# A chunked scan with a split-weight feed-forward: decays of the later units made on TensorE from refilled stacked rows, first outputs of a cell one step later, combination from step 25

## The chip, the cores and the metric

One NeuronCore of a Trainium2 chip runs the whole program. Its engines are named as the profile names them: PE (TensorE matmuls, with PEld for the weight loads), DVE (VectorE), ACT (ScalarE), POOL (GpSimd) and SP (SyncE, which here issues all transfers). The metric is the device time of one execution in microseconds (us). Three runs of the kernel before gave a median of 390.32 us.

## The reference

The inputs are drawn at random: x of shape (4, 8, 768, 32), a decay a between 0.85 and 0.95 for each batch, head and token, B and C with 16 states, and two weight matrices of 256x2048 and 2048x256. The scan works in chunks; between chunks it carries a state. Then every token's 256 values go through two matrix products with a leaky ReLU between them.

```python
log_a = np.log(np.clip(a, 1e-06, 1.0))
for c in range(nc):
    cum = np.cumsum(la, axis=-1)
    L = np.exp(cum[:, :, :, None] - cum[:, :, None, :]) * causal
    M = np.einsum('bhin,bhjn->bhij', Cc, Bc) * L
    y_intra = np.einsum('bhij,bhjd->bhid', M, xc)
    y_inter = np.einsum('bhin,bhnd->bhid', Cc, state) * np.exp(cum)[..., None]
    y[:, :, sl] = y_intra + y_inter
    state = decay_full[:, :, None, None] * state + np.sum(Bx, axis=2)
h = x @ w_in
g = np.maximum(0.01 * h, h)
out = g @ w_out
```

## The kernel before

**Units.** The kernel cuts the sequence into 8 chunks of Q = 96 tokens. One chunk of one batch entry, with its 8 heads, is a unit; there are 32, numbered chunk by chunk. A unit needs its decay tile `lt` (112 x 8 heads x 96: the exponentials of differences of cumulative sums, zero above the diagonal), the score products of B and C (multiplied into `lt` on DVE), the products of `lt` with `xs` that give its output, and, but in the last chunk, the products of `xs` with `bn` that give the next state. ACT copies the state out of PSUM (`stage`), and POOL writes it in four small copies into the rows of the next chunk's `xs`.

**Decays in three ways.** Units 0 to 2 use products of masked logarithms (`decay_direct`). Units 3 to 15 use `decay_pe`: two bf16 matmuls of 384 columns multiply stacked rows `dl` and `dr`. These rows hold a mask and the cumulative sums split in three bf16 parts; the sums come from the DRAM buffer `parts_d` into eight slots (`decay_load`). ACT takes the exponential from PSUM. Units 16 to 31 use another chain: SP broadcasts rows of cumulative sums from the DRAM buffer `crow_d` to all partitions (`decay_rows`), POOL subtracts the column values `ccol` (`decay_sub`, line 270), ACT takes the exponential and POOL zeroes what is above the diagonal (`decay_exp`, lines 278 and 279).

**Three stages.** First come 16 units by themselves. The second stage has 32 steps, which do the feed-forward of the first two of the six tiles of 512 tokens. A step is one block f of 128 hidden columns for one tile: `ffn_in` (line 509) has six matmuls of 512 columns, ACT applies the activation twice (`gh` rounded, `hp` in place), DVE takes the difference (`gl`, line 522), and three steps later `ffn_out` (line 533) accumulates six matmuls in PSUM. The steps form six cells; at a cell's end the sums are added to `ob` on DVE, which frees the two PSUM banks for the next cell's first `ffn_out`. The same steps also decode the weights: `decode` issues two or three DVE passes a step (`PASSES`), five passes and two ACT operations for each of the 16 blocks, and `ffn_in` of a block needs its `wh` and `wl`. At the steps in `PAIR` a `pair_block` does the products of the two earlier units and the scores of two new ones in two PSUM tiles of the pool `ps_c`. The third stage (`two_tiles`, from about 200 us on) does the other four tiles by pairs with a seven-product scheme; `combine` prepares its operands on DVE and POOL.

**Order.** All engines run their instructions in the order in which the program is written. Within a step that order is: rows, subtractions and exponentials of coming units (`early`), `ffn_in`, the second activation, the due decode casts, `gl`, the pair block, the decode passes, the combination, `ffn_out`.

Of the kernel before, what the change touches and what calls it, by code (L numbers as in the profile page):

```python
# [32 lines left out]
WARM = 4  # L33
WARM2 = 4
RAWS = 4
# [23 lines left out]
def scan_ffn(ctx: ExitStack, tc: tile.TileContext, a_l, bc_l, bn_l, x_l, w_l, out_l):  # L59
# [10 lines left out]
    plt = scan.enter_context(tc.tile_pool(name="plt", bufs=6, side="right"))  # L70
# [115 lines left out]
    ccol = const.tile([QE, ncols], F32, name="ccol")  # L186
    erev = const.tile([QE, ncols], F32, name="erev")
    crow = const.tile([128, 2, Q], F32, name="crow")
    parts = const.tile([128, 3, Q], BF16, name="parts")
    crow_d = dram.tile([ncols, Q], F32, name="crow_d")  # L190
    parts_d = dram.tile([128, 3, Q], BF16, name="parts_d")
# [6 lines left out]
    def split_sums(prow):  # L198
        rest = const.tile([128, Q], F32, name="rest")
        nc.tensor.matmul(prow, lhsT=la[:, :128], rhs=upto[:, :Q], start=True, stop=True)  # L200
        nc.vector.tensor_copy(parts[:, 0], prow)
        nc.vector.tensor_tensor(out=rest, in0=prow, in1=parts[:, 0], op=ALU.subtract)
        nc.vector.tensor_copy(parts[:, 1], rest)
        nc.vector.tensor_tensor(out=parts[:, 2], in0=rest, in1=parts[:, 1], op=ALU.subtract)


    def late_sums(one, two):
        for g in range(2):
            nc.tensor.matmul(
                one[:, g * Q:(g + 1) * Q], lhsT=la[:, g * 128:(g + 1) * 128],  # L210
                rhs=upto[:, :Q], start=True, stop=True,
            )
        nc.scalar.copy(crow.rearrange("p g i -> p (g i)"), one[:, :2 * Q])
        nc.sync.dma_start(crow_d.rearrange("(g p) i -> p g i", g=2), crow)
        columns(ccol, upto, AF.Copy, two)
# [31 lines left out]
    def decay_pe(u, space):  # L247
        b = (u - DIRECT) % SLOTS
        for g in range(2):
            nc.tensor.matmul(  # L250
                heads_of(space, g), lhsT=dl[:KD, b], rhs=dr[:KD, b, 4 * g:4 * g + 4],
                start=True, stop=True,
            )
        decay_of(u, space)

    def decay_of(u, space):
# [3 lines left out]
        )  # L260

    def decay_rows(u):
        lt = lts[u] = plt.tile([QE, NH, Q], F32, name="lt")
        rows = crow_d[u * NH:(u + 1) * NH, :].rearrange("r i -> (r i)")
        nc.sync.dma_start(
            lt.rearrange("p h i -> p (h i)"), rows.unsqueeze(0).to_broadcast([QE, NH * Q])
        )

    def decay_sub(u):
        nc.gpsimd.tensor_tensor(  # L270
            out=lts[u], in0=lts[u],
            in1=ccol[:, u * NH:(u + 1) * NH].unsqueeze(2).to_broadcast([QE, NH, Q]),
            op=ALU.subtract,
        )

    def decay_exp(u):
        lt = lts[u]
        nc.scalar.activation(lt, lt, AF.Exp)
        nc.gpsimd.affine_select(  # L279
            out=lt[:Q], in_=lt[:Q], pattern=[[0, NH], [1, Q]], compare_op=ALU.is_ge,  # L280
            fill=0.0, base=0, channel_multiplier=-1,
        )
# [121 lines left out]
    const.tile([128, 336], F32, name="shift0")  # L404
    w_half = [const.tile([128, NF, 2 * DM], F32R, name=n) for n in ("wh", "wl")]
    wh, wl = w_half
    const.tile([128, 416], F32, name="shift")
# [144 lines left out]
    with tc.tile_pool(name="ps_d", bufs=2, space=PSUM, reuse_waits="tile") as ps_d:  # L552
# [15 lines left out]
        split_sums(first[:, 0, :Q])  # L568
        nc.sync.dma_start(parts_d, parts)
# [17 lines left out]
        for u in range(FIRST_UNITS):  # L587
            if u == FIRST_UNITS - 1:
                leads.close()
                pg = ctx.enter_context(tc.tile_pool(name="pg", bufs=LAG + 1))  # L590
# [15 lines left out]
            if v == PE_DECAY - SLOTS - 1:  # L606
                decay_load(DIRECT + SLOTS, PE_DECAY - DIRECT - SLOTS)
            rest()
            c, b = divmod(u, NB)
            if c + 2 <= PE_DECAY // NB:  # L610
# [3 lines left out]
                if b == 2:  # L614
                    fetch_bc(c + 2)
                    fetch_w(c + 1)
                if b == 3:
                    fetch_bn(c + 2)
            if b == 2 and c + 1 < PE_DECAY // NB:
                state_decay(c + 1)  # L620
# [11 lines left out]
    early, late = {}, {}  # L632
# [6 lines left out]
    for u, b in PAIR.items():  # L639
        pair_at[b] = ((u - 2, u - 1) if u > PE_DECAY else (), (u, u + 1))  # L640
# [5 lines left out]
    for c in range(PE_DECAY // NB, NC):  # L646
        b = PAIR[NB * c]
        if NB * c > PE_DECAY:
# [39 lines left out]
    def combine(pair, pools, temps, rhs):  # L688
# [7 lines left out]
        nc.vector.tensor_copy(ab[0][0], a)  # L696
        nc.vector.tensor_tensor(out=t12[:, 0], in0=b[:, 0], in1=a[:, 0], op=ALU.subtract)
        nc.vector.tensor_tensor(out=t34[:, 0], in0=b[:, 1], in1=b[:, 0], op=ALU.subtract)
        nc.gpsimd.tensor_tensor(out=ab[0][1], in0=a, in1=ab[0][0], op=ALU.subtract)
        yield  # L700
        nc.vector.tensor_tensor(out=t12[:, 1], in0=b[:, 1], in1=t12[:, 0], op=ALU.subtract)
        nc.vector.tensor_tensor(out=t34[:, 1], in0=a[:, 1], in1=t12[:, 1], op=ALU.subtract)
        nc.vector.tensor_copy(ab[1][0], b[:, 1])
# [198 lines left out]
```

## Time and profile before

| What | us |
|---|---|
| three runs | 386.65, 390.32, 392.08 |
| the profiled execution, its own time | 390.14 |
| its span, first to last instruction | 388.4 |
| PE busy in the span | 340.4 (88%) |
| DVE busy | 261.3 (67%) |
| ACT busy | 191.0 (49%) |
| POOL busy | 187.4 (48%) |

The page's second part cuts the span in 40 equal slices. Its digits are the busy tenths of each slice, and PEclk is the granted TensorE clock in tenths of full speed. Read the two rows together: where PE shows a 4 or a 5, it waited, and where PEclk falls below 9, it also ran slower.

```profile
PE   7999975998679589579599599999999999999995
PEclk9999995999969879869899899999999999999999
```

The slices from the sixth to the twenty-third are the second stage and the first group of the third.

### The profile page before, as it was taken

Reading aid. Unit: us, or ns where it says so; the run is one execution under the profiler, and the core shown is the slowest. Engines: PE = TensorE matmul, PEld = TensorE weight load, DVE = VectorE, ACT = ScalarE, POOL = GpSimd, SP = SyncE. Lnnn points to the kernel's source line nnn. Section 1 sums busy time; section 2 is a strip of 40 time slices with the busy share of each in tenths; the row PEclk is TensorE's granted clock in tenths of the full one; section 3 lists DMA queues with packets and bytes.
Section 4 is the critical chain, followed back from the end, with each engine's and each line's share of the span. In section 5 each row is a group of like instructions: output and inputs, shape, how many; then the busy total and the mean of one; then the engine's idle time right before and its main releaser. Section 6 shows DMA issues by size and latency. Waiting matters only on the chain.

```text
span 388.4 us, 6367 instructions
## 1 busy us (share of the span) xinstructions
PE 340.4 (88%) x2393; PEld 252.5 (65%) x2393; DVE 261.3 (67%) x379; ACT 191.0 (49%) x365; POOL 187.4 (48%) x268
## 2 busy tenths in 40 slices
PE   7999975998679589579599599999999999999995
PEld 3556543766457468357477477777777787777774
DVE  5349868787877867924866768777666766766552
ACT  3247665355356446423325155554556565566542
POOL 5137875417636728630451638555444555544200
PEclk9999995999969879869899899999999999999999
DMA  5727842392462560000100100000000200000002
GB/s 175 212 86 267 259 146 75 106 296 77 181 194 73 190 183 8 2 0 0 45 11 1 54 2 1 0 2 0 0 2 0 108 3 1 0 3 0 0 2 108
DMA packets 10366, 27.86 MB, mean 72 GB/s; under 512 B 2047, under 2 KB 2271, under 8 KB 10335
## 3 DMA queue, kind: packets, MB, share of 16 engines
q1 hardware_dynamic: 10334, 27.45, 21.6%
q8 instruction: 19, 0.31, 0.3%
q14 instruction: 13, 0.10, 0.1%
HBM read 24.13 MB, written 3.32 MB: 71 GB/s over the span
## 4 chain that ended last, share of the span: by engine, by line
PE 44%; DVE 15%; POOL 4%; issue 3%; ACT 3%; DMA 1%; POOLq 0%; DVEq 0%; ACTq 0%
PE sc L719 15%; PE sc L738 10%; PE op L738 6%; PE hp L719 5%; PE hp L509 4%; PE op L533 3%; DVE u L799 3%; DVE c L800 3%; POOL xs L357 2%; DMA lt<-crow_d 1%; POOL lt L270 1%; DVE wl L450 1%; DVE ob L541 1%; DVE gl L522 1%; POOL lt L279 1%
## 5 line engine op out<-in xcount | busy, mean ns | idle before, releaser
L686 POOL TENSOR_TENSOR sl<-s,sh 128x512 fp32r<-128x512 f32 x16 | 20.9, 1304 | 91.6 <-ACT sh L685 91.6
L751 DVE TENSOR_TENSOR gl<-c,gh 128x512 fp32r<-128x512 f32 x48 | 44.7, 934 | 9.4 <-PE op L738 6.1
L747 ACT ACTIVATE gh<-c 128x512 fp32r<-128x512 f32 x48 | 30.4, 633 | 41.6 <-DVE c L800 18.0
L357 POOL COPY xs<-stage 16x64 f32<-16x64 f32 x112 | 34.8, 311 | 29.7 <-ACT stage L354 22.1
L522 DVE TENSOR_TENSOR gl<-hp,gh 128x512 fp32r<-128x512 f32 x30 | 20.6, 687 | 36.9 <-ACT hp L519 36.7
L533 PE MATMUL op<-gh,wh 128*128 128x512 f32 x64 | 28.4, 443 | 13.6 <-DVE ob L541 12.9
L270 POOL TENSOR_TENSOR lt<-lt,ccol 112x768 f32<-112x768 f32 x16 | 25.1, 1570 | 26.7 <-DMA lt<-crow_d 14.5
L509 PE MATMUL hp<-xh,wh 128*128 128x512 f32 x60 | 26.2, 437 | 9.6 <-ACT wh L443 5.8
L509 PE MATMUL hp<-xh,wl 128*128 128x512 f32 x60 | 26.7, 444 | 9.0 <-DVE wl L450 7.0
L516 ACT ACTIVATE gh<-hp 128x512 fp32r<-128x512 f32 x30 | 17.7, 592 | 31.1 <-PE hp L509 31.1
L748 ACT ACTIVATE c<-c 128x512 f32<-128x512 f32 x48 | 30.4, 633 | 1.5
L719 PE MATMUL sc<-xh,sh 128*128 128x512 f32 x64 | 25.9, 404 | 4.8 <-DVE u L792 4.8
L747 ACT ACTIVATE gh<-hp 128x512 fp32r<-128x512 f32 x16 | 9.6, 598 | 40.9 <-PE hp L719 40.9
L799 DVE TENSOR_TENSOR u<-sc,kept 128x512 f32<-128x512 f32 x16 | 11.1, 692 | 27.6 <-PE sc L719 27.6
L533 PE MATMUL op<-gh,wl 128*128 128x512 f32 x64 | 26.9, 421 | 0.0
L533 PE MATMUL op<-gl,wh 128*128 128x512 f32 x64 | 26.8, 419 | 0.0
L671 POOL TENSOR_TENSOR w<-wh,wl 128x512 f32<-128x512 f32 x16 | 26.5, 1656 | 0.0
L309 DVE TENSOR_TENSOR lt<-sc,lt 112x384 f32<-112x384 f32 x32 | 16.3, 550 | 14.6 <-PE sc L304 11.2
L533 PEld LDWEIGHTS op<-gh,wh 128*128 128x128 f32 x64 | 13.1, 204 | 19.9 <-issue 6.4
L719 PE MATMUL sc<-xl,sh 128*128 128x512 f32 x64 | 25.3, 396 | 0.6 <-DVE xl L709 0.6
L738 PE MATMUL sc<-gh,wh 128*128 128x512 f32 x64 | 25.2, 393 | 0.5 <-DVE ob L732 0.5
L738 PE MATMUL op<-gh,wh 128*128 128x512 f32 x64 | 25.4, 397 | 0.0
(160 smaller groups left out, 921.4 us busy)
## 6 DMA issues: line engine op xcount, KB each, us to landing
raw<-w_l SPq DMA_DIRECT2D x16, 512.0 KB, 3.7
lt<-crow_d SPq DMA_DIRECT2D x16, 336.0 KB, 5.2
bc<-bc_l SPq DMA_DIRECT2D x8, 608.0 KB, 5.0
xs<-x_l SPq DMA_DIRECT2D x8, 384.0 KB, 5.2
out_l<-ob SPq DMA_DIRECT2D x12, 256.0 KB, 2.0
bn<-bn_l SPq DMA_DIRECT2D x8, 231.0 KB, 5.1
la<-a_l SPq DMA_DIRECT2D x1, 96.0 KB, 1.9
crow_d<-crow SPq DMA_DIRECT2D x1, 96.0 KB, 1.9
```

The source lines that it names most:

```text
L270: nc.gpsimd.tensor_tensor(out=lts[u], in0=lts[u], in1=ccol[:, u * NH:(u + 1) * NH].unsqueeze(2).to_broadcast([QE, NH, Q]), op=ALU.subtract,)
L357: nc.gpsimd.tensor_copy(to[:, :, hh], stage[hh * D:hh * D + N])
L509: nc.tensor.matmul(hp, lhsT=w_half[half][:, f, k * 128:(k + 1) * 128], rhs=x[t][:, k, :], start=(n == 0), stop=(n == 5),)
L522: nc.vector.tensor_tensor(out=gls[s], in0=hps.pop(s), in1=ghs[s], op=ALU.subtract)
L533: nc.tensor.matmul(op, lhsT=w_half[half][:, f, DM + m * 128:DM + (m + 1) * 128], rhs=x, start=(first and i == 0), stop=(last and i == 2),)
L671: nc.gpsimd.tensor_tensor(out=w32, in0=wh[:, 2 * p:2 * p + 2, :DM], in1=wl[:, 2 * p:2 * p + 2, :DM], op=ALU.add,)
L719: nc.tensor.matmul(bank, lhsT=w[h], rhs=x[g], start=start and i == 0, stop=i == 2, skip_group_check=True,)
L738: nc.tensor.matmul(outs[t][m], lhsT=w_half[half][:, f, DM + m * 128:DM + (m + 1) * 128], rhs=x, start=first and i == 0, stop=last and i == 2,)
L747: nc.scalar.activation(gh, h, AF.Prelu, alpha=0.01)
L748: nc.scalar.activation(in_place, h, AF.Prelu, alpha=0.01)
L751: nc.vector.tensor_tensor(out=gl, in0=g, in1=gh, op=ALU.subtract)
L799: nc.vector.tensor_tensor(out=u3, in0=B, in1=kept, op=ALU.add)
```

## The change

The second chain of decays goes away. `crow_d`, `crow`, `ccol`, `late_sums`, `decay_rows`, `decay_sub` and `decay_exp` are removed. The cumulative sums of all 32 units are split in bf16 parts at the start, in operations twice as wide, and go to a `parts_d` of twice the size. All units from 3 on use `decay_pe`; after each fourth unit, `decay_load` refills its four slots of `dl` and `dr` from DRAM. For units 16 to 31 `pair_decays` issues the four matmuls and two exponentials one step before the pair block, in the two tiles of `ps_c`.

All pair blocks come two steps earlier, the last one and the combination three steps earlier. In a step the decode passes now stand before the pair block. The first `ffn_out` of a cell (but the first cell) is held for one step and issued with the next one. `combine` no longer uses POOL: DVE does the subtractions, ACT the rounding copies. The pools change: `plt` from 6 to 4 buffers, raw weights from 4 to 3, `pg` from 4 to 5; the two spacer tiles become one of 448 columns. Two more dummy matmuls stand at the start and four more before the first `decay_direct`.

```diff
-WARM = 4
+WARM = 6
-RAWS = 4
+RAWS = 3
+SHIFT = 448
+LOAD = 4
-PE_DECAY = 16
-PAIR = {16: 4, 18: 7, 20: 10, 22: 13, 24: 16, 26: 19, 28: 22, 30: 25}
-LAST_OUT = 28
-COMBINE = 28
+PAIR = {16: 2, 18: 5, 20: 8, 22: 11, 24: 14, 26: 17, 28: 20, 30: 23}
+LAST_OUT = 25
+COMBINE = 25
...
-    plt = scan.enter_context(tc.tile_pool(name="plt", bufs=6, side="right"))
+    plt = scan.enter_context(tc.tile_pool(name="plt", bufs=4, side="right"))
...
     def split_sums(prow):
...
+                prow[:, g], lhsT=la[:, g * 128:(g + 1) * 128], rhs=upto[:, :Q],
+                start=True, stop=True,
...
         decay_of(u, space)
+        after_u = u + SLOTS - LOAD + 1
+        if (u - DIRECT + 1) % LOAD == 0 and after_u < NU:
+            decay_load(after_u, min(LOAD, NU - after_u))
...
-        nc.sync.dma_start(parts_d, parts)
+        nc.sync.dma_start(parts_d.rearrange("(g r) t i -> r g t i", g=2), parts)
...
+        keep_warm(second[:, 1], WARM2)
         decay_direct(0, pds[0])
         decay_of(0, pds[0])
         columns(erev, after, AF.Exp, second[:, 0])
-        late_sums(second[:, 1], first[:, 1])
...
-                pg = ctx.enter_context(tc.tile_pool(name="pg", bufs=LAG + 1))
+                pg = ctx.enter_context(tc.tile_pool(name="pg", bufs=LAG + 2))
...
+    def pair_decays(u):
+        spaces = [score_tile(), score_tile()]
+        for e in range(2):
+            decay_pe(u + e, spaces[e])
...
-        for e in range(2):
-            at(early, b - 4 + e, decay_rows, u + e)
-            at(early, b - 3 + e, decay_sub, u + e)
-            at(early, b - 2 + e, decay_exp, u + e)
+        at(decays, b - 1, pair_decays, u)
...
-        nc.vector.tensor_copy(ab[0][0], a)
+        nc.scalar.copy(ab[0][0], a)
...
-        nc.gpsimd.tensor_tensor(out=ab[0][1], in0=a, in1=ab[0][0], op=ALU.subtract)
...
+        nc.vector.tensor_tensor(out=ab[0][1], in0=a, in1=ab[0][0], op=ALU.subtract)
...
         ffn_low(s)
+        decode(n)
         if s in pair_at:
             pair_block(*pair_at[s])
-        decode(n)
+        for f, args in decays.get(s, ()):
+            f(*args)
...
         if s >= LAG:
-            ffn_out(s - LAG)
+            outs_due.append(s - LAG)
+        if rested or not outs_due or steps[outs_due[0]] not in firsts or outs_due[0] == 0:
+            while outs_due:
+                ffn_out(outs_due.popleft())
+            rested = False
+        else:
+            rested = True
```

Three places show how the order moves. In the rows, the names stand for tiles, with a number for each buffer; the line is that of the helper which issues the row.

ACT, between two pair blocks of the second stage, before: a row with `lt` as output and input is the exponential of one unit, whose input POOL has just subtracted.

```order
L359 COPY x32_1143<-sc_1098 128x2x96
L545 COPY ob0_1163<-op_972 128x512
L278 ACTIVATE lt_1054<-lt_1054 112x768
L516 ACTIVATE gh_1180<-hp_1173 128x512
L519 ACTIVATE hp_1173<-hp_1173 128x512
L412 ACTIVATE w32_1189<-raw_947 128x512
L278 ACTIVATE lt_1082<-lt_1082 112x768
L516 ACTIVATE gh_1212<-hp_1205 128x512
```

The same stretch of ACT now, from the end of one pair block to the step before the next.

```order
L333 COPY x32_1095<-sc_1198 128x2x96
L489 ACTIVATE gh_1269<-hp_1262 128x512
L492 ACTIVATE hp_1262<-hp_1262 128x512
L416 CAST wh_142<-w32_1132 128x512
L489 ACTIVATE gh_1298<-hp_1291 128x512
L492 ACTIVATE hp_1291<-hp_1291 128x512
L385 ACTIVATE w32_1307<-raw_1130 128x512
L254 ACTIVATE lt_1314<-sc_1310 112x768
L254 ACTIVATE lt_1320<-sc_1311 112x768
L489 ACTIVATE gh_1335<-hp_1328 128x512
```

The two exponentials no longer stand ahead of the activations of two steps, waiting for POOL; they stand together, behind a step's activations, and read PSUM tiles that PE fills.

DVE around the pair block, before: `gl` of the step, four multiplications of scores into `lt`, then two decode passes.

```order
L522 TENSOR_TENSOR gl_1092<-hp_1084,gh_1091 128x512
L394 TENSOR_TENSOR lt_951<-sc_1097,lt_951 112x384
L394 TENSOR_TENSOR lt_981<-sc_1097,lt_981 112x384
L394 TENSOR_TENSOR lt_951<-sc_1098,lt_951 112x384
L394 TENSOR_TENSOR lt_981<-sc_1098,lt_981 112x384
L423 TENSOR_SCALAR w32_1072<-w32_1072 128x512
L450 TENSOR_TENSOR wl_143<-w32_1014,wh_142 128x512
```

DVE around a pair block now, with a step of three decode passes.

```order
L495 TENSOR_TENSOR gl_1186<-hp_1178,gh_1185 128x512
L403 SCALAR_TENSOR_TENSOR w32_1132<-raw_950,w32_1132 128x512
L410 SCALAR_TENSOR_TENSOR w32_1132<-raw_950,w32_1132 128x512
L390 TENSOR_SCALAR w32_1194<-w32_1194 128x512
L368 TENSOR_TENSOR lt_1161<-sc_1197,lt_1161 112x384
L368 TENSOR_TENSOR lt_1165<-sc_1197,lt_1165 112x384
L368 TENSOR_TENSOR lt_1161<-sc_1198,lt_1161 112x384
L368 TENSOR_TENSOR lt_1165<-sc_1198,lt_1165 112x384
```

The decode passes moved ahead of the four multiplications, for which ACT's copies of `stage` and `x32` wait.

PE at the first output of the second cell, before: the last `ffn_in` row of a step and the cell's first `ffn_out` rows, into the banks `op_1192` and `op_1193`, which the cell before must have left.

```order
L509 MATMUL hp_1173<-xl_445,wh_142 128x512
L533 MATMUL op_1192<-gh_1038,wh_142 128x512
L533 MATMUL op_1192<-gh_1038,wl_143 128x512
L533 MATMUL op_1192<-gl_1039,wh_142 128x512
L533 MATMUL op_1193<-gh_1038,wh_142 128x512
```

PE at the same output now: the scores of the pair block, then the next step's `ffn_in`, then the cell's first output.

```order
L359 MATMUL sc_1198<-bc_966 112x192 x4
L482 MATMUL hp_1262<-xh_443,wh_142 128x512
L482 MATMUL hp_1262<-xh_443,wl_143 128x512
L482 MATMUL hp_1262<-xl_444,wh_142 128x512
L482 MATMUL hp_1262<-xh_443,wh_142 128x512
L482 MATMUL hp_1262<-xh_443,wl_143 128x512
L482 MATMUL hp_1262<-xl_444,wh_142 128x512
L506 MATMUL op_1277<-gh_1041,wh_142 128x512
```

Six matmuls and the pair block moved between the end of the old cell and the first output of the new one.

More of the change, by code (lines that the diff above doesn't have):

```diff
@@ L184, in scan_ffn @@
     nc.vector.tensor_copy(upto_b, upto)
-    ccol = const.tile([QE, ncols], F32, name="ccol")
     erev = const.tile([QE, ncols], F32, name="erev")
[L188 to L191, printed above, removed]
+    parts = const.tile([128, 2, 3, Q], BF16, name="parts")
+    rest = const.tile([128, 2, Q], F32, name="rest")
+    parts_d = dram.tile([ncols, 3, Q], BF16, name="parts_d")
     def columns(to, mask, func, space):
@@ L198, in split_sums @@
     def split_sums(prow):
[L199 to L207, printed above, removed]
         for g in range(2):
             nc.tensor.matmul(
-                one[:, g * Q:(g + 1) * Q], lhsT=la[:, g * 128:(g + 1) * 128],
-                rhs=upto[:, :Q], start=True, stop=True,
-            )
-        nc.scalar.copy(crow.rearrange("p g i -> p (g i)"), one[:, :2 * Q])
-        nc.sync.dma_start(crow_d.rearrange("(g p) i -> p g i", g=2), crow)
-        columns(ccol, upto, AF.Copy, two)
+                prow[:, g], lhsT=la[:, g * 128:(g + 1) * 128], rhs=upto[:, :Q],
+                start=True, stop=True,
+            )
+        nc.vector.tensor_copy(parts[:, :, 0], prow)
+        nc.vector.tensor_tensor(out=rest, in0=prow, in1=parts[:, :, 0], op=ALU.subtract)
+        nc.vector.tensor_copy(parts[:, :, 1], rest)
+        nc.vector.tensor_tensor(
+            out=parts[:, :, 2], in0=rest, in1=parts[:, :, 1], op=ALU.subtract
+        )
     lts = {}
```

64 lines of the change are left out of this document (22 added, 42 removed).

## The prediction

> **What bounds it.** I read the windows by stage first. Their columns are the stretch, its length, and the busy time of PE, PEld, DVE, ACT and POOL (with instruction counts), then the granted clock.
>
> ```profile
> core 0: us, PE busy (x) PEld busy (x) DVE busy (x) ACT busy (x) POOL busy (x), PEclk, DMA share, GB/s
> 69.00:200.70 131.70, 106.29 (x911) 80.48 (x912) 93.31 (x129) 60.17 (x124) 66.55 (x91) 0.90 0.30 98
> 50.00:69.00 19.00, 11.93 (x63) 7.74 (x63) 13.92 (x20) 10.26 (x20) 11.85 (x20) 0.73 0.39 123
> 200.70:388.40 187.70, 175.61 (x739) 137.76 (x737) 122.81 (x163) 95.97 (x164) 82.23 (x87) 0.99 0.04 15
> ```
>
> The third stage is nearly all PE (175.6 of 187.7 us, clock 0.99). The second stage from its fifth step on (69 to 200.7) is not: PE stands still for 131.7 - 106.3 = 25.4 us, and the clock is 0.90. So the stage is bound by what PE waits for. The waits name it, for PE and then for ACT between 50 and 205 us (total, times, longest):
>
> ```profile
> PE op L533 <- DVE ob L541: 12.9, 3, 5.6
> PE hp L509 <- DVE wl L450: 7.0, 6, 2.5
> ```
>
> ```profile
> ACT lt L278 <- POOL lt L270: 22.1, 12, 3.0
> ACT stage L354 <- DVE lt L394: 16.7, 11, 3.3
> ```
>
> PE waits for DVE (weights, and `ob` that frees the banks), but DVE isn't full, and ACT waits 22.1 us for POOL's subtractions. The groups by line in that stretch show POOL's share and a stretched DVE pass:
>
> ```profile
> L270 POOL TENSOR_TENSOR lt<-lt,ccol 112x768 f32<-112x768 f32 x14 | 22.1, 1576 | 25.5 <-DMA lt<-crow_d 13.4 <-PE sc L385 5.9 <-PE op L533 4.1
> L357 POOL COPY xs<-stage 16x64 f32<-16x64 f32 x48 | 16.2, 337 | 11.2 <-ACT stage L354 6.3 <-issue 2.8
> L279 POOL TENSOR_SCALAR_AFFINE_SELECT lt<-lt 96x768 f32<-96x768 f32 x14 | 14.1, 1010 | 9.1 <-ACT lt L278 7.7 <-DVE w L417 1.0
> ```
>
> ```profile
> L437 DVE SCALAR_TENSOR_TENSOR w<-raw,w 128x512 uint32<-128x512 uint32 x11 | 13.9, 1265 | 0.4
> ```
>
> One case from the timeline, start and duration first: POOL waits 6.66 us for the rows from DRAM, ACT's exponential waits for POOL, the step's activation stands behind it, and `gl` comes 3.87 us late.
>
> ```profile
> 86.81 1.47 POOL L270 TENSOR_TENSOR lt<-lt,ccol 112x768 f32<-112x768 f32 x1 [6.66 <-DMA lt<-crow_d]
> ```
>
> ```profile
> 88.31 0.85 ACT L278 ACTIVATE lt<-lt 112x768 f32<-112x768 f32 x1 [2.54 <-POOL lt L270]
> 89.06 0.58 ACT L516 ACTIVATE gh<-hp 128x512 fp32r<-128x512 f32 x1
> ```
>
> ```profile
> 90.16 0.69 DVE L522 TENSOR_TENSOR gl<-hp,gh 128x512 fp32r<-128x512 f32 x1 [3.87 <-ACT hp L519]
> ```
>
> The second cost of POOL is on DVE. A pass beside POOL's subtraction takes 2.69 us; passes beside POOL's small copies take 0.42 and 0.68.
>
> ```profile
> 74.85 2.69 DVE L437 SCALAR_TENSOR_TENSOR w<-raw,w 128x512 uint32<-128x512 uint32 x1
> ```
>
> ```profile
> 75.53 1.47 POOL L270 TENSOR_TENSOR lt<-lt,ccol 112x768 f32<-112x768 f32 x1
> ```
>
> ```profile
> 114.19 1.95 DVE L394 TENSOR_TENSOR lt<-sc,lt 112x384 f32<-112x384 f32 x4 [1.50 <-issue]
> 116.05 0.42 DVE L423 TENSOR_SCALAR w<-w 128x512 uint32<-128x512 uint32 x1
> 116.39 0.68 DVE L450 TENSOR_TENSOR wl<-w,wh 128x512 fp32r<-128x512 f32 x1
> ```
>
> ```profile
> 115.63 3.48 POOL L357 COPY xs<-stage 16x64 f32<-16x64 f32 x8 [2.80 <-issue]
> ```
>
> Last the clock. After a wait of 2.01 us, matmuls start 0.24 us apart; after one of 3.74 us they start 0.43 apart.
>
> ```profile
> 56.39 0.50 PE L509 MATMUL hp<-xh,wl 128*128 128x512 f32 x1 [2.01 <-POOL wl L472]
> 56.72 0.40 PE L509 MATMUL hp<-xl,wh 128*128 128x512 f32 x1
> 56.96 0.39 PE L509 MATMUL hp<-xh,wh 128*128 128x512 f32 x1
> ...
> 61.56 0.80 PE L509 MATMUL hp<-xh,wh 128*128 128x512 f32 x1 [3.74 <-ACT wh L443]
> ...
> 63.84 0.63 PE L509 MATMUL hp<-xl,wh 128*128 128x512 f32 x1
> 64.27 0.63 PE L509 MATMUL hp<-xh,wh 128*128 128x512 f32 x1
> ```
>
> **The change, part by part.** The sum is made against the profiled execution: span 388.4, its time 390.14, so 1.74 lie around the span. It stands 0.2 under the median of 390.32.
>
> *Second stage, from 69 us.* At the slow clock I count some 44 feed-forward matmuls, between these two, each 0.20 us late:
>
> ```profile
> 107.87 0.79 PE L509 MATMUL hp<-xh,wl 128*128 128x512 f32 x1 [2.54 <-DVE wl L450]
> ```
>
> ```profile
> 195.07 0.56 PE L509 MATMUL hp<-xh,wh 128*128 128x512 f32 x1
> ```
>
> That is 8.8 us, and one pair block, which takes 1.9 at full speed (from its first products to the next output) and 3.3 here, adds 1.4:
>
> ```profile
> 80.12 0.54 PE L321 MATMUL sc<-lt,xs 112*32 112x96 f32 x16
> ...
> 82.04 0.50 PE L533 MATMUL op<-gh,wh 128*128 128x512 f32 x1
> ```
>
> Together 10.2; 0.10 x 131.7 = 13.2 bounds it from above. PE's work at full speed is so 106.3 - 10.2 = 96.1. The 14 units 18 to 31 now add two decay matmuls each:
>
> ```profile
> L250 PE MATMUL pd<-dr,dl 123*112 123x384 bf16 x26 | 7.3, 363 | 0.0
> ```
>
> Two in a row can't cost more than 2 x 0.36 us a unit (10.2 in all), nor less than 384/512 of a spacing of 0.23 (4.8). They follow each other without a wait, so I take the lower end with a little for switching: 5.5. SP loses its broadcasts from 52 us on and gets six refills, three of them here; a refill is issued once PE has used the four slots, and is needed six steps later, at least 6 x 12 x 0.23 = 16 us. That hides it; without this cover it would be a landing of some 4 us. ACT's exponentials stay as many and as long; they lose the wait for POOL. POOL loses L270 and L279 (36.2 of its 66.6 us in the stretch), and with them goes the stretching of DVE: L437 alone lost 11 x (1.27 - 0.69) = 6.4.
>
> What is late next? (a) A weight block that is decoded in the step before its use. For block 9, `ffn_in` of step 13 ends, two activations take 1.2, `gl` 0.69, two passes 0.42 and 0.68: 3.0 us, and DVE comes up to 0.7 later from the steps before. PE has meanwhile only the decays (0.8), since the cell's first output is held: the hold, which is meant against the 12.9 us, costs a wait of up to 2.8 here. Block 14 the same way: 0.7. Block 15 needs two passes, ACT's cast (0.6) and one more pass behind four multiplications: 2.7. (b) The new order on DVE: decode passes ahead of the multiplications delay ACT's `stage` copies, and behind these stands the next step's activation. From one pair block to the next, three steps on, ACT's path is 1.2 + 0.69 + 1.5 (passes) + 1.95 (multiplications) + 0.5 (copies), then 2 x 1.2 for two steps, 1.3 for decode operations and 2 x 0.85 for exponentials: some 11.2 us, an estimate. PE needs 36 x 0.23 + 1.9 + 0.8 + 0.4 = 11.4. That is a tie; I take 2 us in all. (c) Slow clock after such waits: 1. Together 9; bounds are 3 (PE always fed) and 20. The hold's own gain, the 12.9, is part of the 25.4. Result: 96.1 + 5.5 + 9 = 110.6 for 131.7, a gain of 21.1.
>
> A rule beside (c): the Trainium skill (TensorE: Matmul & The Clock Gate, Part 1) has the array's clock halve after about 3.4 us of idleness. The rows with 2.01 and 3.74 agree. By that rule my waits, none over 2.8, would cost no slow clock, and the sum would be 1 us less.
>
> *50 to 69 us.* PE waits here for the first weights. The decays of unit 17 need the PSUM tile in which step 1's activations lie, so step 2 starts some 2 us later; the decode chain loses POOL's stretching and sets the end. I take 0, between -4 (PE waits 7.1 in the 19) and +3.
>
> *Start.* PE loses the sums that only the old chain needed:
>
> ```profile
> 9.56 1.17 PE L209 MATMUL sc<-upto,la 96*128 96x96 f32 x4 [0.47 <-ACT erev L196]
> ...
> 10.52 1.09 PE L195 MATMUL sc<-la,upto 96*112 96x256 f32 x2
> ```
>
> They hold it from 9.56 to about 11.5. Four dummies before `decay_direct` give 0.9 to 1.7 back (0.23 or 0.43 each), the second matmul of the split a little more. The doubled DVE splits and the larger store end long before the first stacked decays at unit 3. I take -0.5, between -2 and +1.
>
> *Third stage.* At its second group, DVE adds two `ob`, copies, subtracts, and is caught by POOL's subtraction:
>
> ```profile
> 213.58 1.28 DVE L541 TENSOR_TENSOR ob<-op,ob 128x512 f32<-128x512 f32 x2
> ...
> 215.98 2.83 DVE L698 TENSOR_TENSOR x<-x 128x512 f32<-128x512 f32 x1
> ```
>
> ```profile
> 215.54 2.72 POOL L699 TENSOR_TENSOR xl<-x,xh 128x1024 fp32r<-128x1024 f32 x1 [4.28 <-DVE xh L696]
> ```
>
> ```profile
> 219.46 0.80 PE L719 MATMUL sc<-xh,sh 128*128 128x512 f32 x1 [4.31 <-DVE u L792]
> ```
>
> Before `u` DVE now has two `ob` and two subtractions of 0.69, 2.7 us where it had 1.28 + 2 x 0.68 + 2.83 = 5.5. So the wait of 4.31 falls to 1.5, and eight matmuls at the slow clock (1.6) go too: -4.4. The five later groups exchange POOL's subtractions for DVE's of 1 to 1.4 us, and ACT gets a copy of about 1.2 ahead of `kept` (an estimate, twice 0.6 for twice the columns); PE has other products in between. I take -4.5 in all, between -6 and +3.
>
> Sum: 388.4 - 21.1 + 0 - 0.5 - 4.5 = 362.3; with 1.74 the time is 364.0.
>
> **Rivals.** *ACT and DVE take over.* The tie of (b) breaks: each of some seven three-step periods takes 1 to 2.5 us more than PE needs. For it speak ACT's 16.7 us behind the multiplications, against it that two `hp` buffers let PE run a step ahead. It gives 364 + 7 to 17 = 371 to 381.
>
> *The change doesn't free DVE.* POOL keeps 66.6 - 40 = 26 us of work in the stretch, with the copies (16.2). If all of it held DVE alike, 26/66 of the 25.4 + 10.2 us would stay: 14, so 378; with all the waits for weights kept as well, 386. The rows at 115.63 and 116.39 speak against it. The Trainium skill (GPSIMD Engine Reference, Key points) speaks for it: GpSimd shares its SBUF interfaces with VectorE and contends with its two-input instructions, whatever GpSimd runs. Here the pass of two inputs at 116.39 took 0.68 beside copies, so the trace bears the rule out for subtractions only.
>
> *Slower: SP's queue.* A refill that waits for PE holds the raw weights behind it.
>
> ```profile
> raw<-w_l SPq DMA_DIRECT2D x16, 512.0 KB, 3.7
> ```
>
> With landings of 3.7 us and 16 us of lead it is hidden. To lose the whole gain of 26 us, each of the three would have to cost PE 9 us, by a landing of over 25. From there on the time is over 390, and 400 at 12 us each.
>
> **How the numbers follow.** Forecast 0.66, with 352 to 371 as its own range. A second stage in which PE is always fed, six of the nine us of waits less and the third stage at its lower bound, gives 364 - 6 - 1.5 = 356 and less: 0.06. ACT and DVE 0.13; DVE not freed 0.12; SP 0.03. The predicted time is the forecast's, 364.0. The range 352 to 378 leaves out some 0.2: most of the third case, the end of the second, the last, and a little below. About 2% is what a measurement of this kernel can tell from no change, so the bounds are 382.5 and 398: faster 0.66 + 0.06 + 0.11 + 0.05 = 0.88, same 0.09, slower 0.03.
>
> **What would show it.** Right: from 69 us to the third stage about 111 us with a clock over 0.95; no wait of PE for `ob` over 1 us; L437's successor at 0.69; a wait near 2.8 us before step 14 and one before step 25; in the third stage no wait over 2 us. Wrong: ACT waiting for multiplications over 20 us (first rival), passes over 1 us beside copies (second), PE waiting for `dl` or `dr` (third).

## The result, and the profile after

The changed kernel takes 352.80 us (median of 352.28 to 353.37), the kernel before 389.31 in the same runs; the ratio is 0.906, with an interval of 0.899 to 0.913. So it is faster by 9.4%, where 6.7% was forecast: the time lies at the lower end of the range of 352 to 378. Runs of one kernel differ by up to 11 us (the kernel before took 381.04 to 392.28 in one set of runs), in part by whether the first 25 us go at full or at half speed, so the ratios given for the later runs compare the quicker runs of both kernels. The changed kernel's median comes from the first set alone, so where a few us matter I compare stage lengths from the profiles. They vary less, but they vary: the third stage, the same program in both, took 183.35 us in the run `pair_first` and 186.11 in `pool_sel`.

The profiled execution of the changed kernel has a span of 351.2 us. The page's row of PE shows where it still waits, in the slices with a 5 or a 7 (the last is the end of the program):

```profile
PE   8999957999979998799979999999999999999995
PEclk9999988899999999899998999999999999999999
```

The windows by stage, of the kernel before and then of the changed one. The stages end where the first `ffn_in` starts, where step 4 starts, where the third stage's first product starts, and at the end of the span.

```profile
0.00:50.15 50.15, 46.62 (x681) 26.49 (x682) 31.43 (x70) 24.64 (x57) 26.90 (x72) 1.00 0.63 198
50.15:68.11 17.96, 11.22 (x63) 7.54 (x63) 12.88 (x18) 10.26 (x20) 11.74 (x19) 0.74 0.36 112
68.11:200.70 132.59, 106.99 (x913) 80.67 (x913) 94.20 (x130) 60.17 (x124) 66.55 (x91) 0.89 0.30 99
200.70:388.40 187.70, 175.61 (x739) 137.76 (x737) 122.81 (x163) 95.97 (x164) 82.23 (x87) 0.99 0.04 15
```

```profile
0.00:42.04 42.04, 39.36 (x683) 23.38 (x683) 31.14 (x70) 24.47 (x55) 27.19 (x73) 1.00 0.72 224
42.04:58.76 16.72, 11.74 (x82) 7.93 (x82) 11.54 (x21) 10.20 (x20) 6.67 (x14) 0.90 0.25 88
58.76:167.21 108.45, 101.60 (x925) 79.64 (x925) 72.87 (x127) 62.91 (x128) 21.38 (x61) 0.97 0.24 81
167.21:351.20 183.99, 175.11 (x739) 137.84 (x737) 124.57 (x160) 98.69 (x168) 81.14 (x85) 0.99 0.04 15
```

| Part | before, us | after, us | measured | predicted |
|---|---|---|---|---|
| start and first units | 50.15 | 42.04 | -8.1 | -0.5 |
| steps 0 to 3 | 17.96 | 16.72 | -1.2 | 0 |
| steps 4 to 31 | 132.59 | 108.45 | -24.1 | -21.1 |
| third stage | 187.70 | 183.99 | -3.7 | -4.5 |
| span | 388.40 | 351.20 | -37.2 | -26.1 |

In steps 4 to 31 PE stands still for 108.45 - 101.60 = 6.9 us where it was 25.6. The waits of PE there (total, times, longest) no longer name `ob` or `gl`; what is left are weights, at four places. The first is the border of step 4, with 0.88 us just ahead of the stretch and 1.00 in it. The timeline shows the other three, the steps 14, 24 and 25 (start and duration first, the wait in brackets).

```profile
PE hp L482 <- ACT wh L416: 3.9, 3, 1.8
PE hp L482 <- DVE wl L423: 3.8, 4, 1.3
```

```profile
98.08 0.49 PE L482 MATMUL hp<-xh,wh 128*128 128x512 f32 x1 [1.22 <-ACT wh L416]
99.90 0.50 PE L482 MATMUL hp<-xh,wl 128*128 128x512 f32 x1 [1.32 <-DVE wl L423]
...
139.03 0.50 PE L482 MATMUL hp<-xh,wl 128*128 128x512 f32 x1 [1.23 <-DVE wl L423]
...
144.99 0.50 PE L482 MATMUL hp<-xh,wh 128*128 128x512 f32 x1 [1.81 <-ACT wh L416]
145.71 0.50 PE L482 MATMUL hp<-xh,wl 128*128 128x512 f32 x1 [0.22 <-DVE wl L423]
```

DVE's groups in the same stretch, after: the pass whose mean was 1265 ns at L437 takes 692 at L410, and `wl`, 1033 ns before, takes 684.

```profile
L403 DVE SCALAR_TENSOR_TENSOR w<-raw,w 128x512 uint32<-128x512 uint32 x11 | 8.5, 774 | 0.0
L423 DVE TENSOR_TENSOR wl<-w,wh 128x512 fp32r<-128x512 f32 x12 | 8.2, 684 | 0.7 <-ACT wh L416 0.7
L410 DVE SCALAR_TENSOR_TENSOR w<-raw,w 128x512 uint32<-128x512 uint32 x11 | 7.6, 692 | 0.4
```

The largest surprise is the start. Here are PE's rows there, first of the kernel before, then of the changed one:

```profile
5.46 2.77 PE L231 MATMUL pd<-lt,after 96*112 96x384 f32 x4
...
18.87 2.77 PE L231 MATMUL pd<-lt,after 96*112 96x384 f32 x4
...
23.93 0.89 PE L250 MATMUL pd<-dr,dl 123*112 123x384 bf16 x2
24.61 0.45 PE L111 MATMUL sc<-idle 128*128 128x512 bf16 x1
25.00 0.59 PE L304 MATMUL sc<-bc 32*112 32x192 f32 x8
```

```profile
5.88 1.28 PE L112 MATMUL sc<-idle 128*128 128x512 bf16 x4
7.00 1.46 PE L224 MATMUL pd<-lt,after 96*112 96x384 f32 x4
...
16.03 0.53 PE L243 MATMUL pd<-dr,dl 123*112 123x384 bf16 x2
```

The same four matmuls of 384 columns take 2.77 us in one kernel and 1.46 in the other. Before, PE ran at half speed until 24.6 us; now until about 6.5, inside the four new dummies (four take 1.28 us here, 1.89 at the start of the kernel before, and 1.03 in the run `best_a`, where they begin at full speed). The granted clock doesn't say so: it reads 1.00 in both first windows above. Here only the duration of one shape, compared between two places, gives the speed away.

### The profile page after: what moved, and what is told of

It reads as the page before. It is cut to its first block, busy times and chain, and to the rows that moved or that the text cites. A ratio compares the mean times of both kernels' runs of the same rounds, so it can differ in the third digit from the quotient of the medians.

```text
span 351.2 us, 6281 instructions
## 1 busy us (share of the span) xinstructions
PE 327.8 (93%) x2427; PEld 248.8 (71%) x2427; DVE 240.1 (68%) x375; ACT 196.3 (56%) x371; POOL 136.4 (39%) x232
## 4 chain that ended last, share of the span: by engine, by line
PE 76%; DVE 15%; ACT 4%; POOL 2%; issue 2%; ACTq 0%; POOLq 0%; DVEq 0%
PE sc L694 17%; PE sc L713 12%; PE hp L482 10%; PE op L506 10%; PE op L713 7%; PE hp L694 6%; DVE u L774 3%; DVE c L775 3%; PE sc L278 2%; PE sc L112 2%; DVE lt L368 2%; PE sc L295 2%; PE pd L295 1%; DVE gl L495 1%; PE sc L243 1%
## 5 line engine op out<-in xcount | busy, mean ns | idle before, releaser
L331 POOL COPY xs<-stage 16x64 f32<-16x64 f32 x112 | 29.7, 266 | 79.3 <-ACT stage L328 52.5
L726 DVE TENSOR_TENSOR gl<-c,gh 128x512 fp32r<-128x512 f32 x48 | 50.3, 1070 | 1.9 <-ACT c L723 1.3
L654 POOL TENSOR_TENSOR s<-w 128x128 f32<-128x128 f32 x32 | 23.5, 736 | 17.5 <-PE sc L295 16.3
L482 PE MATMUL hp<-xh,wh 128*128 128x512 f32 x60 | 24.7, 411 | 4.1 <-ACT wh L416 3.9
L482 PE MATMUL hp<-xh,wl 128*128 128x512 f32 x60 | 24.6, 411 | 4.1 <-DVE wl L423 4.1
L694 PE MATMUL sc<-xh,sh 128*128 128x512 f32 x64 | 25.4, 397 | 2.2 <-DVE u L767 2.2
L506 PE MATMUL op<-gh,wh 128*128 128x512 f32 x64 | 27.1, 424 | 0.0
L713 PE MATMUL op<-gh,wh 128*128 128x512 f32 x64 | 25.4, 397 | 0.0
L713 PE MATMUL op<-gh,wl 128*128 128x512 f32 x64 | 25.4, 397 | 0.0
L713 PE MATMUL op<-gl,wh 128*128 128x512 f32 x64 | 25.4, 396 | 0.0
L506 PE MATMUL op<-gh,wl 128*128 128x512 f32 x64 | 25.3, 395 | 0.0
L506 PE MATMUL op<-gl,wh 128*128 128x512 f32 x64 | 25.1, 392 | 0.0
```

The costliest lines, as they stand in the source:

```text
L331: nc.gpsimd.tensor_copy(to[:, :, hh], stage[hh * D:hh * D + N])
L482: nc.tensor.matmul(hp, lhsT=w_half[half][:, f, k * 128:(k + 1) * 128], rhs=x[t][:, k, :], start=(n == 0), stop=(n == 5),)
L506: nc.tensor.matmul(op, lhsT=w_half[half][:, f, DM + m * 128:DM + (m + 1) * 128], rhs=x, start=(first and i == 0), stop=(last and i == 2),)
L654: nc.gpsimd.tensor_tensor(out=s32[:, i], in0=x, in1=y, op=op)
L694: nc.tensor.matmul(bank, lhsT=w[h], rhs=x[g], start=start and i == 0, stop=i == 2, skip_group_check=True,)
L713: nc.tensor.matmul(outs[t][m], lhsT=w_half[half][:, f, DM + m * 128:DM + (m + 1) * 128], rhs=x, start=first and i == 0, stop=last and i == 2,)
```

## The experiments

**The start.** Three runs ask whether the dummies made the 8 us, or the removal of the sums that PE needed there. First the changed kernel with the dummies of before:

```diff
-WARM = 6
+WARM = 4
-WARM2 = 4
+WARM2 = 0
```

> The changed kernel with its dummies as before (four at the start, none ahead of the first decay_direct). Theory (the dummies bring PE to full speed at 7 us where it came at 24): the products of the first units take twice as long again (the four at decay_direct 2.8 us, not 1.46), the first ffn_in comes near 50 us and not at 42, and the time is 359.5 to 361. Rival (the sums that PE no longer makes at the start, and what waited for them, gave the 8 us): 352 to 354, with decay_direct at 1.46.

Measured: 355.60 us median, but of runs from 352.27 to 360.51. The profiled run is the one of 360.51, and it has the slow start:

```profile
4.29 1.17 PE L199 MATMUL sc<-upto,la 96*128 96x96 f32 x4 [0.49 <-ACT la L533]
...
16.77 2.77 PE L224 MATMUL pd<-lt,after 96*112 96x384 f32 x4
...
48.89 0.50 PE L482 MATMUL sc<-xh,wh 128*128 128x512 f32 x1 [0.16 <-DVE lt L283]
```

So the theory's case came in this run. The other three have no trace, but 352.27 can hardly hold a start that costs 7 us, so it did not come in all. Neither range that I had written is right. By these times the start without the dummies is sometimes slow and sometimes not. Then with the two at the start only:

```diff
-WARM2 = 4
+WARM2 = 0
```

> The changed kernel with six dummies at the start but none ahead of the first decay_direct. If the speed needs work without a gap from 1.3 us on, the two at the start suffice, since they fill the wait of 0.5 us ahead of the sums: 351.5 to 353.5. If it needs the stretch from 5.9 to 7 us filled, the start is slow as before: 358 to 361.

Measured: 350.70 us median (349.67 to 357.39). The profiled run is at full speed some 1.3 us sooner than the changed kernel, and its first `ffn_in` comes at 41.44 and not 42.04. What the four dummies cost where they aren't needed doesn't follow from that, since runs that have them reach the first `ffn_in` between 41.06 (`pool_sub`) and 42.59 (`pair_first`):

```profile
5.18 0.49 PE L217 MATMUL pd<-later,upto_b 96*112 96x384 bf16 x2
5.51 1.45 PE L224 MATMUL pd<-lt,after 96*112 96x384 f32 x4
```

But one run of the four, which has no trace, took 7.7 us more than the quickest. Last the dummies alone in the kernel before:

```diff
-WARM = 4
+WARM = 6
...
+        keep_warm(second[:, 1], 4)
         decay_direct(0, pds[0])
```

> The kernel before with the new dummies alone (six at the start, four ahead of the first decay_direct). Theory (dummies): the first ffn_in comes near 42 to 44 us and the time falls by 6 to 8 to 381 to 384. Rival (late_sums held PE and set the slow start): 389 to 391, or 390 plus the dummies' own 1 us.

Measured: 384.87 us (383.48 to 390.09) against 392.62 for the kernel before, measured beside it, a ratio of 0.980 (0.974 to 0.985). In the profiled run the first `ffn_in` comes at 43.60, and the sums at L209, still there, take 0.69 us after a wait of 0.74. So the dummies bring 7.8 us in the median without any other part of the change, and the sums, which are still there, aren't the cause. With six and four dummies all four runs of the changed kernel lie within 1.1 us; here one of the four took 390.09 us all the same, and has no trace. The profiles of all these experiments say it more plainly: in each of the eleven kernels with six dummies at the start PE reaches full speed between 4.4 and 7.4 us, in the three with four dummies (the kernel before, `start_none`, `hold_before`) between 21.9 and 24.6.

**The hold.** The changed kernel without it:

```diff
-        if rested or not outs_due or steps[outs_due[0]] not in firsts or outs_due[0] == 0:
+        if True:
```

> The changed kernel without the hold: a cell's first output is issued in its own step. Theory (the hold covers the additions of ob): PE waits again for ob at the four later borders of cells, some 2 us each since DVE is freer than before (there 3.3 to 5.6), and gets back the 2.5 us at step 14, where it has outputs to do: 355 to 360. Rival (freeing DVE alone brought the additions in time): 350 to 353, no wait for ob over 1 us.

Measured: 353.02 us (349.67 to 353.44), and 124.99 us from the first `ffn_in` to the third stage where the changed kernel has 125.17. The rival held, nearly: three waits for `ob`, the longest 1.1 us, and in their stead less waiting at step 14 (0.3 us), but 3.2 at step 25 where 1.8 stood. In this kernel the hold brings nothing that these runs show.

```profile
PE hp L482 <- ACT wh L416: 4.9, 3, 3.2
...
PE op L506 <- DVE ob L514: 1.5, 2, 1.1
...
PE op L506 <- DVE ob L520: 0.8, 1, 0.8
```

So I gave the hold to the kernel before, alone (its diff is that of the change, with `pg` at `LAG + 2`):

> The kernel before with the hold alone (and one pg buffer more, which it needs). In the kernel before the stretch from the first ffn_in to the third stage took 150.6 us, with waits for ob of 12.9. If the hold is a cure for late additions of ob, whatever makes them late, those waits go and the stretch falls by 8 to 14 us, weights taking 2 to 4 of it back: 137 to 143 us, time 377 to 384 by the start. If the additions are late because DVE is stretched and the same lateness then shows in the weights, as the run without the hold suggests, the waits move to wh and wl and the stretch stays within 4 us: 147 to 151 us.

Measured: the stretch from the first `ffn_in` to the third stage fell from 150.55 to 190.03 - 49.22 = 140.81 us, by 9.7, as the first theory said. From step 4 on all waits for `ob` went (12.9 before), and waits for weights rose, `wh` from 2.0 to 4.9 and `wl` from 6.1 to 9.0, more than the 2 to 4 us that this theory named:

```profile
PE hp L509 <- DVE wl L450: 9.0, 6, 2.6
PE hp L509 <- DVE gl L522: 5.0, 4, 2.3
PE hp L509 <- ACT wh L443: 4.9, 3, 4.4
```

The medians are 383.61 and 391.37, but the ratio is only 0.990 (0.982 to 0.998). The third stage of the profiled run took 3.4 us more than before (191.07 for 187.70), with a new wait of 2.82 for `xl`. The hold and the rest of the change cure the same lateness, so what each is worth depends on the other: 9.7 us of the stage in the kernel before, nothing in the changed one. That the new decays are what makes the difference is likely by the next runs, but no run adds them alone.

**POOL's work beside DVE.** These two runs put back half of the old decays each, without their waits: POOL works on a tile of its own (it takes the spacer's place), two operations for each pair block, and nobody waits for it.

```diff
-    const.tile([128, SHIFT], F32, name="shift")
...
+    def pool_work():
+        nc.gpsimd.tensor_tensor(
+            out=spare, in0=spare, in1=take.unsqueeze(2).to_broadcast([QE, NH, Q]), op=ALU.subtract,
+        )
...
+        for e in range(2):
+            at(early, b - 1 + e, pool_work)
```

> The changed kernel with sixteen subtractions added on POOL, of the size that the kernel before had there (112 x 768 f32, two inputs), on a tile that nothing else reads or writes. They leave the output as it is, and nothing waits for them. Theory (what the old decays cost was above all DVE's passes stretched beside POOL's subtractions): DVE's decode passes rise from 0.69 towards 1.3 us where they meet, weights and ob come late, and the second stage grows by 5 to 15 us: 358 to 368. Rival (it was the wait of ACT and DVE for POOL's results): the passes may stretch, but the time stays at 352 to 354.

Measured: 365.27 us (364.61 to 365.73), 12.5 more, and 136.75 us from the first `ffn_in` to the third stage, 11.6 more. DVE's groups from step 4 on:

```profile
L402 DVE SCALAR_TENSOR_TENSOR w<-raw,w 128x512 uint32<-128x512 uint32 x11 | 10.9, 987 | 0.0
L422 DVE TENSOR_TENSOR wl<-w,wh 128x512 fp32r<-128x512 f32 x12 | 10.7, 896 | 0.7 <-ACT wh L415 0.7
...
L395 DVE TENSOR_SCALAR w<-w 128x512 uint32<-128x512 uint32 x11 | 7.9, 721 | 0.0
L389 DVE TENSOR_SCALAR w<-w 128x512 f32<-128x512 f32 x11 | 7.1, 649 | 0.0
```

The passes rose from 774 to 987, 684 to 896, 490 to 721 and 420 to 649 ns, and PE waits 9.0 us for `wl` where 4.1 stood. Passes that met no large operation of POOL kept their 0.68 and 0.42 us, so the missing spacer tile isn't the cause, and PE waits for nothing of POOL's. So work on POOL that nobody waits for costs 11.6 us here, nearly half as much as the 25.4 us that this stretch gained: 6.8 of PE standing still (136.75 - 118.17 us, against 125.17 - 113.34), the rest in matmuls that take longer, at a clock of 0.93 for 0.96. Then the selection, with `affine_select` on 96 x 768 in place of the subtraction:

> The same with POOL's other operation of the old decays, the selection of 96 x 768 f32 with one input, on a tile of its own. Theory (only POOL's operations with two inputs hold DVE): DVE's passes stay at 0.42 and 0.69, time 352 to 354. Rival (any POOL work of that size holds DVE): passes stretch as with the subtractions, 356 to 366.

Measured: 360.71 us (358.17 to 363.09, the profiled run), and a stretch of 133.23 us, 8.1 more than the changed kernel. The theory was wrong: an operation with one input holds DVE too.

```profile
L422 DVE TENSOR_TENSOR wl<-w,wh 128x512 fp32r<-128x512 f32 x12 | 10.8, 901 | 0.7 <-ACT wh L415 0.7
L402 DVE SCALAR_TENSOR_TENSOR w<-raw,w 128x512 uint32<-128x512 uint32 x11 | 10.5, 951 | 0.0
...
L395 DVE TENSOR_SCALAR w<-w 128x512 uint32<-128x512 uint32 x11 | 5.3, 486 | 0.0
L389 DVE TENSOR_SCALAR w<-w 128x512 f32<-128x512 f32 x11 | 4.6, 419 | 0.0
```

Passes with two inputs in SBUF are held much as by the subtraction (951 and 901 ns). The means of those with one input (486 and 419) are no higher than in the changed kernel, but only because hardly any met a selection: from step 4 on two of the 22 did. These took 0.83 and 0.77 us, the others 0.41 to 0.43. The first of them, with the selections beside it:

```profile
86.71 1.89 POOL L609 TENSOR_SCALAR_AFFINE_SELECT spare<-spare 96x768 f32<-96x768 f32 x2
87.03 0.83 DVE L395 TENSOR_SCALAR w<-w 128x512 uint32<-128x512 uint32 x1
87.79 1.36 DVE L422 TENSOR_TENSOR wl<-w,wh 128x512 fp32r<-128x512 f32 x1
```

Of the 8.1 us PE stood still for 2.5 (133.23 - 118.94 us, against 11.8); the other 5.6 are matmuls that took longer, at a clock of 0.92 for 0.96.

**The order in a step.** The changed kernel with the pair block ahead of the decode passes:

```diff
-        decode(n)
         if s in pair_at:
             pair_block(*pair_at[s])
+        decode(n)
```

> The changed kernel with the pair block ahead of the step's decode passes, as in the kernel before. Theory (weights are the late part): the passes of pair steps come 1.9 us later, the waits before steps 14, 24 and 25 grow, and the second stage by 1 to 4 us. Rival (ACT's chain behind the multiplications is the late part, my first rival): ACT's copies come 1.1 to 1.8 us earlier and the stage shrinks by 1 to 3 us.

Measured: 355.09 us (354.58 to 357.15, the profiled run), 2.3 more in the median, and a stretch of 129.46 us in the profile, 4.3 more. PE's waits for `wl` total 6.8 where the changed kernel has 4.1, but those for `wh` fell from 3.9 to 2.1. The wait at step 24 grew from 1.23 to 2.55, that at step 14 hardly, and that at step 25 fell. So PE stood still for only 0.8 us more; the other 3.5 are matmuls that took longer, at a clock of 0.92 for 0.96. The theory held for the stretch, which grew and did not shrink: weights are the late part, ACT's copies are not. It did not hold for every wait that it named.

**The combination.** The changed kernel with `combine` of the kernel before (POOL subtracts `xl` of two tiles, DVE makes the rounding copies), from step 25 as now:

> The changed kernel with the combination as it was before (POOL subtracts two tiles, DVE rounds), from step 25 all the same. By the prediction's term the third stage (184.0 us now, 187.7 before) grows by 2.5 to 4.5 us, with a wait for u near 4 us in its second group where 2.2 stands now: 355 to 358. Rival (the combination is hidden beside PE either way, and the term came from the later start): 352 to 354.

Measured: 359.65 us (359.40 to 359.83), 6.9 more and above the 355 to 358 that I had written. Its windows, up to the third stage and in it, and the wait in the second group:

```profile
41.86:170.35 128.49, 114.06 (x1007) 87.40 (x1008) 89.02 (x149) 69.69 (x144) 31.82 (x77) 0.96 0.24 80
170.35:357.70 187.35, 176.11 (x739) 138.78 (x737) 124.55 (x161) 95.73 (x164) 82.28 (x87) 0.98 0.04 15
```

```profile
188.22 0.79 PE L693 MATMUL sc<-xh,sh 128*128 128x512 f32 x1 [4.31 <-DVE u L766]
```

The third stage is 3.4 us longer, with the old wait of 4.31 back in it, as the theory said, and the stretch before it 3.3 us, which I had not foreseen, with a wait of 2.02 for `ob` in its last steps, where the first combination runs.

**What is left in the second stage.** Three decode passes in every step:

```diff
-PASSES = (3,) * 5 + (2, 3) * 10
+PASSES = (3,) * 25
```

> The changed kernel with three decode passes in every step in place of two and three by turns, so that blocks come ready one to three steps earlier. Theory (the five waits for weights from step 13 on, 5.8 us, and the slow clock behind them are all that PE lacks there): waits under 1 us from 66 us to the third stage, the stage 6 to 8 us shorter, 345 to 347 with a start at full speed. Rival (the added passes delay gl and ACT's stage copies, or raw weights come late with three buffers): other waits of 2 us and more, 350 to 355.

Measured: 345.79 us (344.28 to 346.56), 7.0 less than the changed kernel, and a stretch of 118.42 us from the first `ffn_in` to the third stage, 6.8 less. The waits for weights from step 5 on are gone, and with them the slow clock:

```profile
59.37:160.36 100.99, 97.90 (x925) 77.88 (x925) 73.66 (x127) 62.17 (x128) 21.82 (x61) 1.00 0.26 87
```

One new wait came up, 1.35 us at 98.92 for a unit's exponential, as the rival half foresaw. Two further steps on top of it. The first:

```diff
+        ffn_act(0)
+        settle()
+        ffn_low(0)
+        decode(PASSES[0])
         ffn_in(1, hp[:, 1])
...
-    two_tiles(queue, TWOS[0], rhs_of[0], lambda p: next(combining, None))
+    two_tiles(queue, TWOS[0], rhs_of[0], lambda p: next(combining, None) if p else None)
```

> The changed kernel with three decode passes in every step; the whole of step 0 behind its ffn_in (second activation, gl, decode) ahead of the second ffn_in, so that DVE starts on it 2.3 us earlier; and the second combination begun one group later, so that u of the second group has two additions ahead of it and not two additions and two subtractions. Against the run with three passes alone (345.8): 1.5 to 2.5 us from DVE's earlier start, 1.4 of the wait of 2.2 for u and up to 2 of slow clock behind it: 340 to 343. Rival (the waits only move: to the block after, or to the next group): 344 to 346.

Measured: 344.75 us (343.90 to 347.02), in the rival's range. That is 1 us less than with three passes alone, within the spread of both. The third stage of the profile is 2.0 us shorter, the stretch before it unchanged (118.46). The longest wait for `u` in the third stage fell from 2.19 to 1.08 us. The earlier `gl` failed: the two halves of `hp` lie in one PSUM tile, and now PE waits there for step 0's difference before it writes step 1's half.

```profile
46.05 0.77 PE L482 MATMUL sc<-xh,wh 128*128 128x512 f32 x1 [2.37 <-DVE gl L495]
```

The second, with the first pair block a step later:

```diff
-PAIR = {16: 2,
+PAIR = {16: 3,
```

> The same with the first pair block and its decays one step later (steps 3 and 2), so that the decode passes of block 4 come ahead of its four multiplications. If PE waits at steps 2 to 4 for decays and weights of a busy DVE, another 1 to 2 us go: 338.5 to 342. Rival (the next pair block, two steps on, now waits for the first): as the run before or up to 2 us longer.

Measured: 342.21 us (342.00 to 342.99), a ratio of 0.890 (0.884 to 0.895) to the kernel before, and just above the 338.5 to 342 that I had written. Steps 0 to 3 take 15.44 us where the run before it had 58.91 - 41.43 = 17.48. This is the best version of the study, 10.6 us under the changed kernel.

```profile
42.53:57.97 15.44, 11.73 (x83) 8.12 (x83) 11.29 (x18) 9.90 (x20) 6.70 (x14) 0.89 0.27 92
57.97:158.80 100.83, 98.02 (x925) 77.81 (x925) 75.05 (x129) 62.17 (x128) 21.80 (x61) 1.00 0.27 88
158.80:341.30 182.50, 174.25 (x739) 136.59 (x737) 125.72 (x160) 98.59 (x168) 82.44 (x85) 1.00 0.04 15
```

## Why the prediction was right, and where it was off

**The start failed.** The step was "Four dummies before `decay_direct` give 0.9 to 1.7 back", in a term of -0.5 "between -2 and +1". It priced the dummies as work and missed that PE ran at half speed until 24.6 us. The rows quoted for that step had it in them: 1.09 us for two matmuls of 256 columns, where the same two take 0.61 in the run with the new dummies. I took the clock of 1.00 for the first 50 us at its word. The term was -8.1 in the profile and -7.8 in the run with the dummies alone. That is most of the 11 us by which the sum was off. It was luck that a term 7.6 us off, and far outside its own bounds, left the time 0.8 us inside the range.

**Steps 4 to 31: the mechanism right, the terms somewhat off.** By the prediction's own cut (0.11 us ahead of step 4's second matmul) the stretch went from 131.7 to 167.21 - 60.15 = 107.1 us, for 110.6 forecast. The waits came where they were said to: before step 14, 1.22 + 1.32 = 2.5 for up to 2.8; at step 24, 1.23 for 0.7; before step 25, 2.0 for 2.7. The 2 us for a tie of ACT and DVE didn't come. PE's work, taken from the run with three passes (clock 1.00, the same matmuls: 99.6 us by that cut, less 2.1 of waits), is 97.5 and not 96.1 + 5.5 = 101.6. Of the 4.1, one score block of 0.9 moved ahead of the cut, which I didn't count; the decays took some 4.5, by 0.51 us for four matmuls and 0.13 of switching, seven times; what is left, about 2, I put down to slow clock of the kernel before beyond the 10.2 that I had counted, which was not measured by itself. Slow clock after the remaining waits was 107.1 - 97.5 - 5.9 = 3.7, not 1. So the 9 us of waits and slow clock came out as 9.6 by errors that cancel.

**The rule on the clock.** By the rule that the prediction weighed (the Trainium skill, TensorE: Matmul & The Clock Gate, Part 1), waits under 3.4 us would cost no speed. Here matmuls come 0.43 us apart after waits of 1.81 and 0.22, so the trace doesn't bear it out. The same section says that the window runs free of the kernel's start, and that the change to full speed therefore varies by half a microsecond from run to run. The starts vary too, but by far more: the changed kernel and those that begin like it came to full speed between 4.4 and 7.4 us, and the three with four dummies not before 21.9.

**The hold and DVE.** That the hold's gain was "part of the 25.4" was right for the sum and wrong as an attribution: it is worth 9.7 us in the kernel before and nothing in the changed one. That POOL's operations on decays stretch DVE's passes, and that this costs PE time, is shown by the two runs with POOL's work put back: 11.6 and 8.1 us of stretch, 6.8 and 2.5 of them with PE standing still. How the whole gain of this stretch divides between that, ACT's waits for POOL and the new order isn't shown, since no run gives the kernel before the new decays alone.

**The rivals.** ACT and DVE did not take over: ACT's waits behind the multiplications were 17.4 us, under the 20 named, and giving them room cost 4.3 us of stretch. SP's refills were hidden; PE waited for no `dl` or `dr`. The second rival went the way of the forecast here, since POOL keeps only small copies, but my sentence that the trace bears out the rule on GpSimd "for subtractions only" was too narrow. The Trainium skill (GPSIMD Engine Reference, Key points) names contention for VectorE's instructions with two inputs in SBUF and for those in a 2-port mode; it sets no condition on what GpSimd runs. The selections agree for the passes with two inputs (901 ns in the mean for 684). They held passes with one input too (0.83 us for 0.42); whether these ran in a 2-port mode, no run here shows. Beside the small copies the pass of 0.68 us stays an exception.

**Third stage and steps 0 to 3.** -3.7 for -4.5: the wait for `u` fell to 2.17 us and not to 1.5, over the 2 us that I had set for this stage, and eight matmuls behind it came 0.43 us apart. The run with the old combination gives 3.4 for the term. In steps 0 to 3 the second unit's decays waited 3.58 us, not 2, and by the trace for the first unit's exponential, not for step 1's activations; the old waits of 2.01 and 3.74 went, so 1.2 us were gained where 0 was forecast.

## What to carry to other kernels

Compare the duration of one shape of matmul between places of a trace before you believe the clock's row; a start at half speed cost 7 to 8 us here, far more than the dummies that ended it (four take 1.0 to 1.6 us of PE). Two cures for one lateness don't add: when a change frees the engine that is late, try without the detour that was built around it. A mean over all passes doesn't tell what a neighbour does to them: look at the ones that met it. And once an engine has room, give it its work earlier: three decode passes a step were worth 7 us more, since DVE stood still for a third of the stage.

## What the runs showed of the hardware

- PE can stay at half speed for some 20 us of matmuls that follow each other without a wait that the trace shows (4.3 to 24 us in the run without the new dummies), though another run of the same kernel was 8 us quicker, by its time without such a start. With six dummies at the start all eleven profiles show full speed by 7.4 us, with four all three profiles show it only from 21.9 us on or later. What exactly decides it stays open.
- The granted clock reads 1.00 throughout such a start, while later slow stretches show in it (0.74, 0.90).
- GpSimd's selection with one input slows DVE passes with two inputs in SBUF (684 to 901 ns in the mean) and, where it meets them, passes with one input (0.42 us to 0.77 and 0.83); its subtraction slows both (to 1.45 us and more for passes with one input that met it). DVE's difference `gl`, which reads PSUM, kept its 0.69 us in all of these runs, also beside such work.
